# Moving one pair of token blocks of a two-layer GLU kernel into the joint seven-product stage

## The chip and the metric

One core of a Trainium2 chip. Times are microseconds of the device for one execution; runs of the same kernel are compared by their median.

## The reference

Channel attention on (6016, 256) tokens, then two gated layers with 1536 hidden units:

```python
def _attn_ref(q, k, v, tau):
    qn = q / (np.linalg.norm(q, axis=1, keepdims=True) + 1e-06)
    kn = k / (np.linalg.norm(k, axis=1, keepdims=True) + 1e-06)
    s = kn.transpose(0, 2, 1) @ qn / tau
    ...
    return (v @ a).astype(np.float32)

def _moe_ref(x, w_gate, w_val, w_out, rms_g):
    rms = np.sqrt(np.mean(x * x, axis=-1, keepdims=True) + 1e-06)
    xn = x / rms * rms_g
    g = xn @ w_gate
    silu = g * (1.0 / (1.0 + np.exp(-g)))
    val = xn @ w_val
    return (silu * val @ w_out).astype(np.float32)

def _moe2_ref(x, w_gate, w_val, w_out):
    gate = 1.0 / (1.0 + np.exp(-(x @ w_gate)))
    val = x @ w_val
    return (gate * val @ w_out).astype(np.float32)
```

## The kernel before, in words

The head computes the 256x256 attention matrix and multiplies the tokens by it. After that the program is two GLU layers on 12 blocks of 512 tokens (block 5 has 384), with hidden tiles f = 0 to 11 of 128 units. Every product is three fp32r matmuls of a high and a low half (`mm3`), so high and low halves of operands and weights are made on ScalarE ("hi": a copy) and VectorE ("lo": a difference).

Blocks go in pairs p = 0 to 5; the two halves of a pair are 512 tokens wide, those of pair 2 448. Three kinds of work stand in the program one after the other:

- **Plain**: 48 items (block, f) for blocks 0 to 3, the pairs 0 and 1 of layer one. An item has gate and value products in the banks `g` and `v` (12 matmuls, `plain_gv`), the output products of the item two before (6 matmuls, `out_mm`), and on the other engines gate, multiply, hi and lo (`plain_h`). The two layers' weights arrive as 64-bit floats and are converted here, 24 tiles (l, f), in the steps `units`, `shifted`, `whole`, `signed`, `size`, `rounded`, `guarded`, `high`, `low`, then `sums` of weight blocks on POOL with their own halves `s_high`, `s_low`, and stores to DRAM. `queue` lays the steps out after the table `ORDER` (a name with "-" is a step of the tile before), and `pump` puts a few behind each item's own work; `quota` says how many.
- **Alone** (`period`): pair 2 of layer one. A period is one f: the eight gate and value block products are made by seven, named 11, S1, P4, T2, 12, T3, S4, with copies of banks between them on ScalarE, and the output is made plainly by four products: 11 products, 33 matmuls. Weights stay in SBUF (`wh`, `wl`).
- **Joint** (`team_period`): pairs 3, 4, 5 of layer one, then pairs 0, 1, 3, 4, 5, 2 of layer two. The gate and value products are made as above. For the output, six hidden tiles make a team (half a pair); it takes 21 products (7 kinds x 3) for 24, made during the next half pair (`out_product`). So the first half pair, periods 0 to 5, has no output work (the step list `NONE`), and later ones have 10.5 products a period (`EVEN`, `ODD`). Weights are fetched from DRAM by `gw_load` (gate, value) and `ow_load` (output), operands by `pair_load`.

The program is in the order in which it is written (`manual_schedule`): each engine takes its instructions one after the other, DMAs are issued by SP, and accumulating DMAs by POOL. In the joint stage the step lists set the order: "cpA", "e5", "cpG", "cpD" are ScalarE's copies of banks, "sg" and "gate" its activations, "h1", "h0", "g1", "v1" VectorE's work. T3 writes to the bank that "cpG" reads, so T3 waits for "cpG".

Of the kernel before, what the change touches and what calls it, by code (L numbers as in the profile page):

```python
# [17 lines left out]
P = 128  # L18
SKEW = 2
# [6 lines left out]
def kernel(  # L26
# [35 lines left out]
    PLAIN = 2  # L62
    p0 = [starts[2 * p] * P for p in range(NP)]
# [37 lines left out]
    s3d = [dram.tile([P, 2, P], F32, name=f"s3d{f}") for f in range(NF)]  # L101
# [20 lines left out]
    def six(t):  # L122
        return t[:, A11:].rearrange("p (m c) n -> p m c n", c=KC)

    def conversion(l, f):
# [45 lines left out]
        def sums():  # L171
            t = w["t"]
            nc.sync.dma_start(out=rd[l][f // 2][:, f % 2 * 2 : f % 2 * 2 + 2], in_=t[:, OUT:])
            w["s3"] = cv2.tile([P, 1, P], F32, tag="s3", name="s3")
            nc.gpsimd.tensor_add(t[:, S1], t[:, A21], t[:, A22])
            nc.gpsimd.tensor_sub(w["s3"][:, 0], t[:, A11], t[:, A21])
# [3 lines left out]
        def high():  # L180
            if l:
                h = cv2.tile([P, NG, P], F32R, tag="w2h", name="w2h")
            else:
                h = wp.tile([P, NQ, P], F32R, tag=f"wh{f}", name="wh")
            own = slice(A11, NG if l else NQ)
            nc.scalar.copy(h[:, own], w["t"][:, own])
            w["h"] = wh[l, f] = h

        def low():
            if l:  # L190
                lo = cv2.tile([P, NG, P], F32R, tag="w2l", name="w2l")
            else:
                lo = wp.tile([P, NQ, P], F32R, tag=f"wl{f}", name="wl")
            own = slice(A11, NG if l else NQ)
            nc.vector.tensor_sub(lo[:, own], w["t"][:, own], f32(w["h"][:, own]))
            w["l"] = wl[l, f] = lo

        def sums_high():
            h = w["h"]
            nc.scalar.copy(h[:, :A11], w["t"][:, :A11])  # L200
            if l:
                w["3h"] = h[:, S3 : S3 + 1]
            else:
                w["3h"] = cv1.tile([P, 1, P], F32R, tag="s3h", name="s3h")
            nc.scalar.copy(w["3h"], w["s3"])

        def sums_low():
            h, lo = w["h"], w["l"]
            nc.gpsimd.tensor_sub(lo[:, :A11], w["t"][:, :A11], f32(h[:, :A11]))
            if l:  # L210
                w["3l"] = lo[:, S3 : S3 + 1]
            else:
                w["3l"] = cv1.tile([P, 1, P], F32R, tag="s3l", name="s3l")
            nc.gpsimd.tensor_sub(w["3l"], w["s3"], f32(w["3h"]))

        def stored():
            if l:
                nc.sync.dma_start(out=gd[l][f][:, 0], in_=f32(w["h"]))
                nc.sync.dma_start(out=gd[l][f][:, 1], in_=f32(w["l"]))
                del wh[l, f], wl[l, f]  # L220
            else:
                nc.sync.dma_start(out=s3d[f][:, 0], in_=f32(w["3h"])[:, 0])
                nc.sync.dma_start(out=s3d[f][:, 1], in_=f32(w["3l"])[:, 0])
# [6 lines left out]
        "-high units shifted", "-low", "whole signed", "size -s_high -s_low rounded", "guarded sums -stored"  # L230
# [3 lines left out]
    def queue(first, late):  # L234
# [7 lines left out]
        for i, tile_of in enumerate([*conversions, None]):  # L242
# [3 lines left out]
            for group in ORDER:  # L246
# [8 lines left out]
            if i + 2 < len(conversions):  # L255
                steps[-1].append(partial(load_w, *conversions[i + 2]))
# [135 lines left out]
    def pair_load(l, p, own):  # L392
# [8 lines left out]
        for i, (c, e) in ((B11, (0, 0)), (T3, (0, 1)), (B22, (1, 1)), (B21, (1, 0))):  # L401
# [39 lines left out]
    def plain_gv(it):  # L441
        b, f = it
        w = sizes[b] * P
        gv[it] = [gv_bank("g"), gv_bank("v")]
        for m, ps in enumerate(gv[it]):
# [878 lines left out]
```

## Time and profile before

| | |
|---|---|
| runs before | 1170.06 us median of 3 (1167.53 to 1170.07) |
| profiled execution | 1170.04 us, span 1168.3 us |
| TensorE | 1148.7 us busy (98%) |
| VectorE | 968.3 us (83%) |
| ScalarE | 890.2 us (76%) |
| POOL | 334.3 us (29%) |
| granted clock | 0.996 mean |

A timeline row gives start and duration in us, engine, source line, operation, out<-in by tile names, shapes, and in brackets the idle time before it and what ended it. The end of a matmul is modelled, so two starts tell more than one duration. A row by stage gives length, then busy time (and instructions) of TensorE, its weight loads, VectorE, ScalarE and POOL, then granted clock, DMA share and GB/s.

### The profile page before, as it was taken

How to read it: one execution, taken by the hardware profiler on the slowest of the kernel's cores; microseconds unless marked ns; L12 is line 12 of the kernel's file. 1: busy time of each engine (PE TensorE's matmuls, PEld its weight loads, DVE VectorE, ACT ScalarE, POOL GpSimd, SP SyncE). 2: the span in 40 equal slices, each digit the busy share in tenths (PEclk: the TensorE clock that was granted, in tenths of full speed). 3: DMA queues.
4: the chain of work that ended last, by engine and by line, in shares of the span. 5: the costliest groups of instructions: out<-in, count | busy, mean ns of one | idle time of the engine just before them, and what ended most of it. 6: DMA issues, size and time to landing. Idle time of an engine off the chain costs nothing.

```text
span 1168.3 us, 16678 instructions
## 1 busy us (share of the span) xinstructions
PE 1148.7 (98%) x5236; PEld 957.0 (82%) x5236; DVE 968.3 (83%) x1496; ACT 890.2 (76%) x1664; POOL 334.3 (29%) x398
## 2 busy tenths in 40 slices
PE   8899999999999999999999999999999999999998
PEld 7788788888898778888888788888888888888896
DVE  6798999886667688888888887888888888888877
ACT  6666788775577687887787887787787787787685
POOL 0043677454223322321321321311311321321121
PEclk9899999999999999999999999999999999999999
DMA  9663445867489989999999998998998998998995
GB/s 329 241 220 143 145 148 190 282 228 238 145 280 322 355 258 266 303 264 266 303 262 272 300 258 251 287 265 245 288 265 240 293 260 247 293 261 245 284 273 147
DMA packets 142856, 296.84 MB, mean 254 GB/s; under 512 B 13872, under 2 KB 53168, under 8 KB 142768
## 3 DMA queue, kind: packets, MB, share of 16 engines
q1 hardware_dynamic: 122032, 258.65, 65.6%
q0 software_dynamic: 20592, 37.00, 18.1%
q8 instruction: 41, 0.67, 0.2%
q14 instruction: 47, 0.39, 0.1%
q10 hardware_dynamic: 144, 0.13, 0.0%
HBM read 201.98 MB, written 56.75 MB: 221 GB/s over the span
## 4 chain that ended last, share of the span: by engine, by line
PE 84%; DVE 8%; DMA 4%; issue 2%; ACT 2%; POOL 1%; SPq 0%; DVEq 0%; POOLq 0%; ACTq 0%
PE g L107 12%; PE g L109 12%; PE g L108 12%; PE v L107 6%; PE v L108 6%; PE v L109 6%; PE y L108 5%; PE y L109 5%; PE y L107 5%; PE at L108 4%; PE at L107 4%; PE at L109 4%; DMA in<-in_q_dram 1%; PE y L973 1%; DVE xn L329 1%
## 5 line engine op out<-in xcount | busy, mean ns | idle before, releaser
L605 POOL DMA_DIRECT2D hs<-hs x143 | 124.7, 918 | 571.5 <-DVE hl L688 413.6
L688 DVE TENSOR_TENSOR hl<-hs,hh 128x512 fp32r<-128x512 f32 (+1 forms) x319 | 221.1, 704 | 25.1 <-ACT hh L657 24.2
L657 ACT CAST hh<-hs 128x512 fp32r<-128x512 f32 (+1 forms) x319 | 192.6, 615 | 25.7 <-PE at L109 6.5
L874 ACT COPY v<-g 128x512 f32<-128x512 f32 (+1 forms) x210 | 119.0, 567 | 63.1 <-PE g L109 59.8
L879 DVE TENSOR_TENSOR hs<-g,e 128x512 f32<-128x512 f32 (+1 forms) x105 | 71.5, 681 | 66.5 <-ACT v L874 65.6
L107 PE MATMUL g<-xh,gw 128*128 128x512 f32 x240 | 94.1, 392 | 0.7 <-DVE hs L879 0.6
L108 PE MATMUL g<-xl,gw 128*128 128x512 f32 x240 | 93.5, 389 | 0.0
L109 PE MATMUL g<-xh,gw 128*128 128x512 f32 x240 | 93.4, 389 | 0.0
L908 ACT ACTIVATE g<-g 128x512 f32<-128x512 f32 (+1 forms) x108 | 67.5, 625 | 30.4 <-DVE g L912 29.4
L107 PE MATMUL y<-hh,ow 128*128 128x512 f32 (+1 forms) x211 | 81.7, 387 | 0.2 <-issue 0.2
L108 PE MATMUL y<-hl,ow 128*128 128x512 f32 (+1 forms) x211 | 81.7, 387 | 0.0
L109 PE MATMUL y<-hh,ow 128*128 128x512 f32 (+1 forms) x211 | 81.6, 387 | 0.0
L874 ACT COPY g<-g 128x512 f32<-128x512 f32 (+1 forms) x105 | 61.3, 583 | 26.2 <-PE g L109 25.8
L912 DVE TENSOR_TENSOR g<-g,g 128x512 f32<-128x512 f32 (+1 forms) x105 | 70.3, 669 | 5.7 <-PE g L109 5.7
L883 ACT ACTIVATE sg<-v 128x512 f32<-128x512 f32 (+1 forms) x108 | 64.2, 594 | 7.5
L107 PE MATMUL g<-qh,gw 128*128 128x512 f32 (+1 forms) x171 | 66.5, 389 | 0.7 <-DVE hs L879 0.6
L109 PE MATMUL g<-qh,gw 128*128 128x512 f32 (+1 forms) x171 | 65.8, 385 | 0.0
L108 PE MATMUL g<-ql,gw 128*128 128x512 f32 (+1 forms) x171 | 65.8, 385 | 0.0
L108 PE MATMUL at<-hl,ow 128*128 128x512 f32 (+1 forms) x160 | 62.4, 390 | 0.6 <-DVE hl L688 0.6
L107 PE MATMUL at<-hh,ow 128*128 128x512 f32 (+1 forms) x160 | 62.2, 389 | 0.3 <-ACT hh L657 0.2
L109 PE MATMUL at<-hh,ow 128*128 128x512 f32 (+1 forms) x160 | 61.9, 387 | 0.0
L874 ACT COPY e<-g 128x512 f32<-128x512 f32 (+1 forms) x105 | 61.3, 584 | 0.4
(256 smaller groups left out, 3312.4 us busy)
## 6 DMA issues: line engine op xcount, KB each, us to landing
gw<-gd SPq DMA_DIRECT2D x216, 448.0 KB, 5.6
ow<-od SPq DMA_DIRECT2D x126, 384.0 KB, 5.4
hs<-hs POOLq DMA_DIRECT2D x128, 256.0 KB, 7.7
wraw<-in_w_dram SPq DMA_DIRECT2D x24, 768.0 KB, 5.3
od<-o SPq DMA_DIRECT2D x48, 256.0 KB, 4.6
vraw<-in_v_t_dram SPq DMA_DIRECT2D x11, 512.0 KB, 4.9
gd<-w2h SPq DMA_DIRECT2D x12, 448.0 KB, 2.6
gd<-w2l SPq DMA_DIRECT2D x12, 448.0 KB, 3.6
```

Source lines behind the costliest of these rows:

```text
L107: nc.tensor.matmul(ps, sh, mh, start=start, stop=False, skip_group_check=more)
L108: nc.tensor.matmul(ps, sh, ml, start=False, stop=False, skip_group_check=more)
L109: nc.tensor.matmul(ps, sl, mh, start=False, stop=stop, skip_group_check=more)
L329: nc.vector.tensor_scalar_mul(xn[b][:, i], ps[i // 2][:, i % 2], rs[:, i : i + 1])
L605: nc.gpsimd.dma_start(out=to, in_=t, accum_op=ALU.add)
L657: nc.scalar.copy(h, src)
L688: nc.vector.tensor_sub(lo, src, f32(h))
L874: nc.scalar.copy(new(name, make, *args), s[src])
L879: nc.vector.tensor_add(s["v1"], s["Z"], s["e5"])
L883: nc.scalar.activation(out=new("sg0", lambda: t), in_=s["A"], func=acts[l])
L908: "gate": lambda: nc.scalar.activation(out=pv["g1"], in_=pv["g1"], func=acts[pl]),
L912: "g1": lambda: nc.vector.tensor_add(s["g1"], s["g1"], s["B"]),
```

## The change

All pairs of layer one behind the plain stage become joint, in the order 3, 4, 5, 2; `period` goes. The plain stage therefore has to leave everything in DRAM that the joint stage fetches: gate and value weights (`store_plain`, `stored`), output weights (`store_out`) and the sums of output weights of layer one (`out_load`, `out_sums`, `out_high`, `out_low` behind items 22 to 41); those of layer two's first three pairs of tiles come behind periods 0, 2 and 4 (`soon_halves`). In the conversion the guard of a tile goes behind the next tile's sign step, raw weights have three buffers, and a load is asked for three tiles ahead (`FIRST` and `SECOND`, for the first four tiles that `queue` lays out, hold the old order). The last two plain items' output products run inside period 0 (`plain_out`), their banks are emptied there, and the two stores follow behind period 1. Of the first six periods the even ones use the `y` banks and the odd ones `g` (before: even `g`, odd `at`).

```diff
-    NQ = 9
-    S1, S2, S4, A11, A12, A21, A22, OUT = range(8)
-    S3 = A21
-    NG = OUT
+    NQ = 10
+    S3, S1, S2, S4, A12, A11, A22, A21, OUT = range(9)
+    NS = A12
+    NG = A21
+    NW = NQ - NS
...
-        t = cv2.tile([P, 3, KC, P, 2], U32, tag="wraw", name="wraw")
+        t = cv2.tile([P, 3, KC, P, 2], U32, tag="wraw", name="wraw", bufs=3)
...
     ORDER = (
-        "-high units shifted", "-low", "whole signed", "size -s_high -s_low rounded", "guarded sums -stored"
+        "units shifted",
+        "whole signed",
+        "size load -guarded -sums",
+        "-high rounded",
+        "-low -s_high -s_low -stored",
+    )
...
-            for group in ORDER:
+            if i + 3 < len(conversions):
+                now["load"] = partial(load_w, *conversions[i + 3])
+            for group in FIRST if i < first + 3 else SECOND if i == first + 3 else ORDER:
...
-    alone = [(0, PLAIN, f) for f in range(NF)]
-    joint = [(0, p, f) for p in range(PLAIN + 1, NP) for f in range(NF)]
+    joint = [(0, p, f) for p in (*range(PLAIN + 1, NP), PLAIN) for f in range(NF)]
     joint += [(1, p, f) for p in (0, 1, 3, 4, 5, 2) for f in range(NF)]
-    stream = alone + joint
...
     NONE = (
-        "11 S1 cpA gate h1 P4 third part1 T2 e5 12 flush h0 first"
-        " gw early part0 out out cpG ACT out sg T3 cpD out S4 end"
-        " DVE g1 v1"
+        "11 S1 cpA gate h1 P4 third T2 e5 12 flush h0 first gw early out out cpG ACT out sg T3 cpD out S4 DVE g1 v1 end"
     ).split()
...
         def bank(j):
-            return (at_bank, j) if n < HALF and n % 2 else (gv_bank, "g")
+            return (gv_bank, "g") if n >= HALF or n % 2 else (y_bank, j)
...
-            "S1": lambda: product(new("B", *bank(0)), it, T1, S1, True),
+            "S1": lambda: (product(new("B", *bank(0)), it, T1, S1, True), pv or out()),
...
-        end = len(items) - 5
+        now = len(items) - LATE
+        end = now - 6
+
+        def store_plain(f):
+            for e, t in enumerate((wh[0, f], wl[0, f])):
+                nc.sync.dma_start(out=gd[0][f][:, e, NS:], in_=f32(t[:, : NG - NS]))
+
+        def store_out(f):
+            g, j = divmod(f // 2, NJ)
+            for e, t in enumerate((wh[0, f], wl[0, f])):
+                nc.sync.dma_start(out=od[0][g][:, f % 2 * 2 : f % 2 * 2 + 2, e, j], in_=f32(t[:, 2 * KC :]))
...
+        for u, n in enumerate([22, 25, 28, 31, 34, 37]):
+            hook(n, out_load, 0, u)
+            hook(n + 2, out_sums, 0, u)
+            hook(n + 4, out_high, 0, u, 4)
+            hook(n + 4, out_low, 0, u, 4)
...
+        def plain_out(n):
+            b, f = items[n]
+            for c in range(KC):
+                out_mm(0, b // 2, b % 2, f, c)
+            if f == NF - 1:
+                for c in range(KC):
+                    evacuate(0, b // 2, b % 2, c, c, f32(hidden("hh")), True)
...
+            if n in SOON_AT:
+                slots[0].setdefault("end", []).append(partial(soon_halves, SOON_AT.index(n)))
...
-            if n < len(alone):
-                s = period(it, pv, outs)
-            elif it:
-                s = team_period(it, pv, n - len(alone), outs)
+            if it:
+                s = team_period(it, pv, n)
             else:
-                team_end(pv, n - len(alone))
+                team_end(pv, n)
+            if n == 1:
+                for fn in waiting:
+                    fn()
```

How the instructions stand now, at two places. First VectorE in the plain stage, one conversion and the plain items between (`v<-v,sg` and `hl<-v,hh` are a plain item's multiply and lo; `wbits<-wraw`, `wbits<-wraw,wbits`, `wbits<-wbits,wunits`, `wst<-wst,wbits`, `wl<-wst,wh` are shifted, signed, rounded, guarded, low). Before:

```order
L148 TENSOR_SCALAR wbits<-wraw 128x768
L195 TENSOR_TENSOR wl<-wst,wh 128x768
L478 TENSOR_TENSOR v<-v,sg 128x512
L158 SCALAR_TENSOR_TENSOR wbits<-wraw,wbits 128x768
L480 TENSOR_TENSOR hl<-v,hh 128x512
L163 ISA wbits<-wbits,wunits 128x1536
L166 SCALAR_TENSOR_TENSOR wst<-wst,wbits 128x768
L478 TENSOR_TENSOR v<-v,sg 128x512
```

and now:

```order
L149 TENSOR_SCALAR wbits<-wraw 128x768
L493 TENSOR_TENSOR hl<-v,hh 128x512
L159 SCALAR_TENSOR_TENSOR wbits<-wraw,wbits 128x768
L167 SCALAR_TENSOR_TENSOR wst<-wst,wbits 128x768
L491 TENSOR_TENSOR v<-v,sg 128x512
L164 ISA wbits<-wbits,wunits 128x1536
L493 TENSOR_TENSOR hl<-v,hh 128x512
L195 TENSOR_TENSOR wl<-wst,wh 128x768
```

The guard stood behind its own tile's rounding; now the guard of the tile before stands behind this tile's sign step, and the low half follows this tile's rounding.

Second ScalarE around the first joint period (`hh<-v` is the last plain item's hi, `v<-y`, `e<-y`, `g<-y` are cpA, e5 and cpG of period 0, `sg<-v` its sg, the second `v<-y` cpD). Only the new order has this seam:

```order
L492 CAST hh<-v 128x512
L387 CAST xh<-xl 128x512
L831 COPY v<-y 128x512
L831 COPY e_3353<-y 128x512
L522 COPY hh<-at 128x512
L831 COPY g_3368<-y 128x512
L840 ACTIVATE sg<-v 128x512
L831 COPY v<-y 128x512
L575 CAST o<-o 128x512 x2
L831 COPY v<-g 128x512
```

The emptying of a plain output bank (`hh<-at`) stands between e5 and cpG of period 0, and two splits of output weights (`o<-o`) stand behind its cpD, ahead of period 1's cpA.

## Rows read from the trace of the kernel before

**Rows 1.** First section of the page: busy time, share of the span, instructions.

```profile
PE 1148.7 (98%) x5236; PEld 957.0 (82%) x5236; DVE 968.3 (83%) x1496; ACT 890.2 (76%) x1664; POOL 334.3 (29%) x398
```

**Rows 2.** Busy time by stage, columns as told above.

```profile
387.18:421.81 34.63, 34.24 (x142) 25.84 (x141) 22.29 (x35) 23.47 (x44) 7.15 (x6) 1.00 1.00 341
...
465.19:551.86 86.67, 86.25 (x380) 70.76 (x379) 74.63 (x117) 69.70 (x128) 22.34 (x24) 1.00 0.96 279
1069.43:1109.46 40.03, 40.03 (x191) 35.50 (x190) 33.49 (x57) 29.98 (x58) 6.97 (x8) 1.00 0.95 273
119.00:200.00 81.00, 79.89 (x352) 65.99 (x352) 79.40 (x98) 64.70 (x111) 56.94 (x69) 1.00 0.51 166
200.00:280.00 80.00, 80.00 (x352) 65.72 (x351) 71.14 (x94) 58.74 (x103) 41.80 (x60) 1.00 0.72 246
```

**Rows 3.** Timeline of TensorE: plain matmuls nine apart, and the seventh joint period.

```profile
182.55 0.39 PE L107 MATMUL v<-qh,wh 128*128 128x512 f32 x1
...
184.59 0.39 PE L107 MATMUL at<-hh,wh 128*128 128x512 f32 x1
...
421.81 0.40 PE L107 MATMUL g<-qh,gw 128*128 128x512 f32 x1
```

**Rows 4.** Timeline of TensorE: first alone period's matmuls one and six, and a wait.

```profile
304.23 0.36 PE L107 MATMUL g<-xh,wh 128*128 128x448 f32 x1
...
305.24 0.36 PE L109 MATMUL g<-xh,wl 128*128 128x448 f32 x1
...
313.72 0.37 PE L109 MATMUL v<-xh,wl 128*128 128x448 f32 x1
314.68 0.44 PE L107 MATMUL at<-hh,wh 128*128 128x448 f32 x1 [0.60 <-DVE yo L509]
```

**Rows 5.** Timeline of TensorE and ScalarE in joint period 2: T2's end, cpG, T3.

```profile
402.95 0.39 PE L109 MATMUL g<-qh,gw 128*128 128x512 f32 x1
...
403.63 0.39 PE L109 MATMUL v<-qh,gw 128*128 128x512 f32 x1
404.02 0.50 PE L107 MATMUL g<-zh,gw 128*128 128x512 f32 x1
404.36 0.40 PE L108 MATMUL g<-zl,gw 128*128 128x512 f32 x1
...
403.38 0.59 ACT L874 COPY g<-g 128x512 f32<-128x512 f32 x1 [0.40 <-PE g L109]
```

**Rows 6.** Timeline of ScalarE in joint period 1: emptying of a bank, then cpG.

```profile
397.78 0.55 ACT L507 COPY yo<-y 128x448 f32<-128x448 f32 x1
398.29 0.59 ACT L874 COPY g<-at 128x512 f32<-128x512 f32 x1
```

**Rows 7.** Groups of VectorE from 119 to 200 us: signed, guarded, rounded.

```profile
L158 DVE SCALAR_TENSOR_TENSOR wbits<-wraw,wbits 128x768 uint32<-128x768 uint32 x12 | 12.6, 1047 | 0.0
L166 DVE SCALAR_TENSOR_TENSOR wst<-wst,wbits 128x768 f32<-128x768 f32 x11 | 12.2, 1112 | 0.3
...
L163 DVE CUSTOM_DVE_ANT_0 wbits<-wbits,wunits 128x1536 uint16<-128x1536 uint16 x11 | 10.6, 962 | 0.8
```

**Rows 8.** Timeline: lo of plain items 4, 16, 19; value product two items later.

```profile
130.01 0.68 DVE L480 TENSOR_TENSOR hl<-v,hh 128x512 fp32r<-128x512 f32 x1
...
133.59 0.39 PE L107 MATMUL v<-qh,wh 128*128 128x512 f32 x1
...
181.19 0.68 DVE L480 TENSOR_TENSOR hl<-v,hh 128x512 fp32r<-128x512 f32 x1
...
190.68 0.69 DVE L480 TENSOR_TENSOR hl<-v,hh 128x512 fp32r<-128x512 f32 x1
...
194.79 0.39 PE L107 MATMUL v<-qh,wh 128*128 128x512 f32 x1
```

**Rows 9.** Groups of POOL from 304 to 388 us: first sum of output weights.

```profile
L571 POOL TENSOR_TENSOR o<-o 128x128 f32<-128x128 f32 x9 | 6.4, 713 | 51.7 <-DVE o L563 31.4 <-PE g L109 20.3
```

**Rows 10.** Busy time by stage: the last pair.

```profile
1100.00:1140.00 40.00, 39.95 (x196) 36.27 (x195) 32.07 (x57) 32.41 (x66) 7.83 (x9) 1.00 0.99 281
```

More of the change, by code (lines that the diff above doesn't have):

```diff
@@ L181, in high @@
             if l:
-                h = cv2.tile([P, NG, P], F32R, tag="w2h", name="w2h")
-            else:
[L184 to L187, printed above, removed]
+                h = w["sh"] = cv2.tile([P, NG, P], F32R, tag="w2h", name="w2h")
+                nc.scalar.copy(h[:, NS:], w["t"][:, NS:NG])
+            else:
+                h = wh[l, f] = wp.tile([P, NW, P], F32R, tag=f"wh{f}", name="wh")
+                nc.scalar.copy(h, w["t"][:, NS:])
@@ L216, in stored @@
-        def stored():
[L217 to L223, printed above, removed]
+            if not l:
+                w["sh"] = cv2.tile([P, NG, P], F32R, tag="w2h", name="w2h")
+            h = w["sh"]
@@ new lines, in sums_high @@
+            nc.scalar.copy(h[:, :NS], w["t"][:, :NS])
+        def sums_low():
+            if not l:
+                w["sl"] = cv2.tile([P, NG, P], F32R, tag="w2l", name="w2l")
+            h, lo = w["sh"], w["sl"]
+            nc.gpsimd.tensor_sub(lo[:, :NS], w["t"][:, :NS], f32(h[:, :NS]))
+        def stored():
+            for e, t in enumerate((w["sh"], w["sl"])):
+                if l:
+                    nc.sync.dma_start(out=gd[l][f][:, e], in_=f32(t))
+                else:
+                    nc.sync.dma_start(out=gd[l][f][:, e, :NS], in_=f32(t[:, :NS]))
@@ L229 @@
     ORDER = (
-        "-high units shifted", "-low", "whole signed", "size -s_high -s_low rounded", "guarded sums -stored"
+        "units shifted",
[4 more added lines that the diff above has]
+    )
+    FIRST = (
+        "-high units shifted",
+        "-low",
+        "whole signed",
+        "size load -s_high -s_low rounded",
+        "guarded sums -stored",
+    )
+    SECOND = (
+        "-high units shifted",
+        "-low",
+        "whole signed",
+        "size load -s_high -s_low rounded",
+        "-stored",
     )
@@ L923, in team_period @@
         for step in (EVEN, ODD)[n % 2] if n >= HALF else NONE:
-            do.get(step, partial(at, step))()
+            if pv or step not in ("gate", "h1", "P4", "h0", "first"):
+                do.get(step, partial(at, step))()
         return s
@@ L1230 @@
                 slots.extend({} for _ in range(NF))
-                if n <= len(alone):
-                    done = outs[-1][:2]
-                    for e in range(2) if pv else (1,):
-                        point = slots[0].setdefault("ACT", []) if e and pv else slots[1].setdefault("early", [])
-                        point.extend(partial(evacuate, *done, e, c, c) for c in range(KC))
-                if n + NF < len(stream):
-                    nxt = stream[n + NF][:2]
+                if n + NF < len(joint):
+                    nxt = joint[n + NF][:2]
                     own = ((n // NF) % 2) == 1
@@ L1281 @@
             pv = s
-            outs = [(*it[:2], e, it[2]) for e in (1, 0)] if n < len(alone) else []
 def kernel(**inputs):
```

269 lines of the change are left out of this document (101 added, 168 removed), and 8 rows, old and new, of tables (EVEN, ODD).

## The prediction

> **What bounds the kernel now.** The first section of the page says it: TensorE is busy for nearly the whole span and VectorE is next [rows 1]. So I asked for busy time by stage, to see whether any stage is held by something else [rows 2]. In the plain stage (119 to 280 us) TensorE has no idle time to speak of, with VectorE right behind it, at 79.40 of 81 us in its first part. In a layer-one pair of the joint kind (465.19 to 551.86 us) 378 matmuls of 512 columns take 86.67 us. So the time is the number of matmuls times their spacing, plus the places where TensorE waits. The timeline of TensorE gives the spacing from start to start: 512 columns, 2.04 us over 9 matmuls, 0.2267 us [rows 3]; 448 columns, 1.01 us over 5, 0.202 us [rows 4]; I use 0.2025, since 126 x 0.2025 + 63 x 0.2267 = 39.8 us answers to the 40.03 us of the half pair at 1069.43 us [rows 2]. The granted clock is 1.00 in all these stretches, so no term of mine is one of the clock.
>
> The timeline then shows where layer one pays for more than its matmuls. The first matmul of the "alone" stage (pair 2) starts at 304.23 us [rows 4], the seventh joint period at 421.81 us [rows 3]: 117.58 us. Between them lie 396 matmuls of 448 columns (12 periods of 11 products, three matmuls each), 12 of 512 (output products of the last two plain tiles) and 126 of 512 (six joint periods of 7 products): 396 x 0.2025 + 138 x 0.2267 = 80.2 + 31.3 = 111.5 us. So 6.1 us here are waits, of a kind shown at 314.68 us, where the accumulation of a new output bank waits for the copy that empties it [rows 4].
>
> **The change, part by part.**
> *Products.* Pair 2 leaves the alone stage, is put behind pair 5 and gets its output product by seven for eight as well. Its output matmuls go from 12 x 4 x 3 = 144 to 42 x 3 = 126: 18 fewer, 18 x 0.2025 = 3.65 us. The rule in the Trainium skill, "TensorE: Matmul & The Clock Gate", section "Back-to-back issue gap", gives N/2.4 + 2.5 ns, 189 ns at 448 columns, and would make this 3.4 us; the trace's 202 ns decides.
>
> *The seam from plain to joint.* Now the first joint period follows the last plain tile. Its 138 matmuls of 512 columns cost 31.3 us as before. Of its waits two are readable. In each of the first joint periods T3 waits for the copy of T2's bank, with only "12" between: the last matmul of T2 starts at 402.95 us, the copy at 403.38, T3 at 404.02 in place of 403.86, and its next matmul 0.34 us later in place of 0.23: 0.27 us a period [rows 5]. Five periods keep that, 1.36 us; the bank swap alters which banks, not this chain. In period 0 output work lies between, but ScalarE's program now has the emptying of the last plain output bank ahead of that copy (the second piece of order above). So T3 waits for the last output matmul to drain (0.43 us from its start to the copy's, as at 402.95), for the emptying (0.51 us from its start to the next copy's [rows 6]) and for the copy (0.64 us to T3): 1.58 us instead of 0.23, a wait of 1.35 us. Bounds: nothing, if the copy gets through in time, and 1.9 us, if the emptying on VectorE is late as well by one operation; I take 1.35, since each piece has its row. The stores of these two banks wait for period 1; nobody reads that half of pair 1 until layer two.
>
> *Added to the first periods:* two splits each (1.1 us of ScalarE, 1.4 us of VectorE) behind periods 0, 2 and 4. ScalarE was busy 23.47 of 34.63 us there and VectorE 22.29 [rows 2]; ScalarE's idle 11.2 us over six periods take 3.3 us. I take nothing and keep 0 to 1.0 us.
>
> *Pair 2 as a joint pair:* 378 x 0.2025 = 76.5 us. The layer-one pair at 465.19 us took 86.67 for 378 x 0.2267 = 85.7: 1.0 us of waits [rows 2]. I charge pair 2 the same; bounds 0.2 (the half pair at 1069.43 us, 40.03 for 39.8) and 2.
>
> *The plain stage.* Removed there: the small conversions of S3. Added: splits of the layer-one output sums (6 on VectorE and ScalarE, 24 small POOL sums), stores of weights, DMAs on SP. Moved: the guard of a tile goes behind the next tile's sign step, and the third raw buffer lets a load go out three tiles ahead. VectorE's cover is the thing to check. I counted its operations up to each plain tile's "hl" in both orders, with the means of this stage. They agree up to tile 3; at tile 4 the new order is one guard later, 1.11 us [rows 7], where the old one has a lead of 2.90 us (hl done at 130.69, the bank's next matmul at 133.59) [rows 8]. From 6 to 16 it is equal or earlier by up to 0.26 us; tile 16 has the thinnest lead, 0.68 us (181.87 against 182.55) [rows 3, 8]. At 19 it is 1.83 us late (one more sign step and rounding, 1.05 + 0.96, less 0.18 for a smaller split) against a lead of 3.42 us (191.37, 194.79) [rows 7, 8]. No lead is used up. After 200 us VectorE has 8.9 us of 80 idle [rows 2], and the six splits take 4.1 (0.68 each, as an hl). POOL and SP have no work that TensorE waits for here except through those leads. I take zero, 0 to 2 us.
>
> *The sum.* Old stretch 117.58. New: 31.3 + 1.36 + 1.35 + 0.2 (spacing a little wide in these periods) = 34.2, and 76.5 + 1.0 = 77.5: 111.7. The gain is 5.9 us, 3.65 of it matmuls and the rest waits of the alone stage that go with it. The profiled execution took 1170.04 us (span 1168.3), the median is 1170.06, so both give 1164.1 us. All other pairs, the last one among them, have the same matmuls.
>
> **The rivals.**
> *A seam without the new wait* (the emptying hidden): 1.35 us less and perhaps half of pair 2's waits, 1162.3 us. For it: VectorE has the other bank and ScalarE is idle right before. Against it: the order on ScalarE. Chance 0.12.
>
> *The plain stage loses its lead.* POOL gets 24 sums there, at most 0.71 us each [rows 9], 17 us. If they held VectorE for as long as they run, it would have 17 + 4.1 us more work between 200 and 280 us against 8.9 idle, and end 12 us late against a lead like that of tile 19, 3.42 us: at worst 8.8 us of waits, 1173 us, and at half of that 1168.5, which I take for its time. Against it: between 119 and 200 us POOL was busy 56.94 us and VectorE 79.40 of the same 81 [rows 2], so they ran side by side. The Trainium skill, "SBUF — State Buffer", section "SBUF: two separate sides", says that GpSimd and a VectorE operation with two SBUF inputs lock one another out for a whole instruction; by that this rival would be the likely one, and those two busy times do not bear it out for the mix as a whole. Chance 0.13.
>
> *The seam or the splits cost double:* waits of the first periods as large as those of the alone stage, 6 us instead of 2.9, 1167 us. Chance 0.09.
>
> *The transfers fall behind in pair 2, and it gets slower.* At 448 columns a period is shorter, but its gate and value weights are as many bytes. The last pair moved 281 GB/s [rows 10]; pair 2 has in addition the next pair's operands, four loads of 256 KB in 77 us, 14 GB/s: 295. If the queues hold only R, pair 2 stretches by 77 x (295/R - 1): at 263 GB/s 9.4 us, which is 1173.5. It decides from about there down. Against it: 341 GB/s between 387.18 and 421.81 us, 279 in an ordinary pair, and no wait of TensorE for a weight load in either [rows 2]. Chance 0.05.
>
> *It does not do what it says:* no gain from the moved pair because its waits are as large as the alone stage's; that is inside the third rival.
>
> **How the numbers follow.** Forecast 1164.1 us, chance 0.61, its own range 1162.8 to 1166.2 (the bounds above, not all at their worst). With the first rival below and the second and third above, 1161.8 to 1168.5 holds eight in ten. 0.3% is 3.5 us, about what a measurement can tell: faster means under 1166.6. That takes the forecast nearly whole (0.59), the first rival (0.12) and a little of the others (0.06): 0.77. Slower, over 1173.6: 0.05. The rest, 0.18, is within.
>
> **What would show it.** Right: the stretch from the last plain tile to the seventh joint period is about 34 us; one wait of some 1.3 us before T3 of period 0, put down to a ScalarE copy; pair 2 takes 77 to 78 us; no new TensorE wait between 120 and 300 us. Wrong: TensorE waits for VectorE or a weight in the plain stage; joint periods of pair 2 longer than 6.5 us with waits for "gw" or "ow"; or a matmul spacing that differs from 0.2267 and 0.2025 us for whole stretches.

## The result and the profile after

The changed kernel takes 1177.63 us (median of 4, 1175.63 to 1180.3); the kernel before, run beside it, 1168.8. The ratio is 1.0076, 95% interval 1.0055 to 1.0096: slower by some 9 us, where 1164.1 was forecast, 1166.2 was the top of the forecast's own range and 1168.5 that of the wider one. The profiled execution took 1180.3 us, its span is 1178.5 us, 10.2 more than before. One execution among all the kernels below, one of the seven of the changed kernel without the splits, took 1911 us, and the ratio given there leaves it out.

The first section of its page shows no engine that became the bound: TensorE is at 98% again, with 18 matmuls fewer [rows 1].

```profile
PE 1150.0 (98%) x5218; PEld 955.3 (81%) x5218; DVE 985.2 (84%) x1524; ACT 892.1 (76%) x1654; POOL 339.3 (29%) x390
```

Busy time by stage tells where the 10.2 us are. The columns are those of [rows 2]. Before, the plain stage (first plain product to the first alone one) and the first half of layer two's first pair were:

```profile
104.81:304.23 199.42, 197.43 (x869) 161.49 (x869) 175.48 (x230) 144.46 (x255) 110.50 (x142) 1.00 0.56 185
...
638.64:682.72 44.08, 43.83 (x190) 35.16 (x189) 37.99 (x60) 35.30 (x63) 12.52 (x12) 1.00 0.98 286
```

After: the plain stage (to the first joint product), pair 3's first half, the two halves of pair 2, and layer two's first half pair.

```profile
103.68:316.73 213.05, 203.78 (x868) 162.77 (x869) 180.72 (x234) 142.77 (x237) 120.03 (x150) 0.98 0.78 262
316.73:353.83 37.10, 34.08 (x139) 25.12 (x138) 26.13 (x40) 26.40 (x49) 10.57 (x10) 1.00 0.77 242
570.36:612.08 41.72, 40.31 (x190) 35.41 (x189) 37.22 (x60) 32.09 (x62) 12.93 (x12) 1.00 1.00 298
612.08:650.75 38.67, 38.67 (x191) 35.41 (x190) 31.98 (x58) 32.01 (x65) 7.00 (x8) 1.00 0.97 276
650.75:693.43 42.68, 42.55 (x190) 35.17 (x189) 35.74 (x59) 33.45 (x61) 12.53 (x12) 1.00 0.97 279
```

The plain stage, which I had priced at zero, takes 213.05 us for 199.42: 13.6 us more for the same products. Counted from start to start, 5.1 us of that are waits before value products between 187 and 284 us, 2.9 a single wait at 307.6 us, and 3.0 two stretches at half the clock, shown at the end. The part on which my gain rested, pair 3's first half and pair 2, takes 37.10 + 41.72 + 38.67 = 117.5 us where the old stretch took 117.58 and 111.7 was forecast. The head is 1.1 us shorter, and the rest, layer two's first half pair above all, 2.2 us. 13.6 - 1.1 - 0.1 - 2.2 = 10.2.

**How a wait in the plain stage comes about.** Between 240 and 290 us TensorE stands before the value product of a tile at 242.9, 255.7, 260.9, 270.5 and 283.5 us; its timeline shows two of them:

```profile
255.66 0.39 PE L110 MATMUL g<-qh,wl 128*128 128x512 f32 x1
256.85 0.50 PE L108 MATMUL v<-qh,wh 128*128 128x512 f32 x1 [0.80 <-DVE hl L493]
...
260.87 0.39 PE L110 MATMUL g<-qh,wl 128*128 128x512 f32 x1
262.44 0.50 PE L108 MATMUL v<-qh,wh 128*128 128x512 f32 x1 [1.19 <-DVE hl L493]
```

The value bank is free when hl of the tile ahead is done. So read backwards from hl at 256.11, on VectorE, ScalarE and POOL, in the same microseconds:

```profile
248.86 0.95 DVE L159 SCALAR_TENSOR_TENSOR wbits<-wraw,wbits 128x768 uint32<-128x768 uint32 x1
...
250.32 1.87 DVE L167 SCALAR_TENSOR_TENSOR wst<-wst,wbits 128x768 f32<-128x768 f32 x1
252.92 0.78 DVE L579 TENSOR_TENSOR ol<-o,oh 128x512 fp32r<-128x512 f32 x1 [0.73 <-POOL wst L175]
253.63 1.21 DVE L164 CUSTOM_DVE_ANT_0 wbits<-wbits,wunits 128x1536 uint16<-128x1536 uint16 x1
254.77 0.69 DVE L491 TENSOR_TENSOR v<-v,sg 128x512 f32<-128x512 f32 x1
255.37 0.54 DVE L192 TENSOR_TENSOR w2l<-wst,w2h 128x384 fp32r<-128x384 f32 x1
256.11 0.69 DVE L493 TENSOR_TENSOR hl<-v,hh 128x512 fp32r<-128x512 f32 x1 [0.20 <-ACT hh L492]
257.14 2.24 DVE L390 TENSOR_TENSOR ql<-ql,qh 128x512 fp32r<-128x512 f32 x2 [0.34 <-ACT qh L387]
```

```profile
251.42 0.91 ACT L137 ACTIVATE wst<-wraw 128x768 f32<-128x768 f32 x1 [1.10 <-POOL w2l L207]
252.23 0.61 ACT L575 CAST oh<-o 128x512 fp32r<-128x512 f32 x1
```

```profile
248.96 1.17 POOL L595 TENSOR_TENSOR o<-o 128x128 f32<-128x128 f32 x1
250.09 1.30 POOL L207 TENSOR_TENSOR w2l<-wst,w2h 128x512 fp32r<-128x512 f32 x1
```

POOL makes the low part of a tile's sums until 251.39. ScalarE's size step (L137) of the tile two further needs the buffer that this reads (there are two), so it stands 1.10 us. Behind it in ScalarE's line is `oh`, the rounding of a split output sum; VectorE's guard ends at 252.19, but `ol`, next in its line, needs `oh`, which ends at 252.84: VectorE is idle for 0.73 us. (The row names POOL L175 as the releaser; that started at 252.28 and ended no earlier than 252.7, so what `ol` waited for is `oh`.) Rounding, product, hh and hl follow in line, and TensorE waits 0.80 us by its row, 0.96 by its starts. One tile on, two subtractions of the next block (2.24 us) meet the lateness that is left, 1.19 us. At 283.5 us the same three instructions stand in the same order; at 270.5 us ScalarE waits for POOL at another place, the rounding of the sums (L201, 0.82 us), again with `oh` next in line. The small wait at 242.9 us, 0.21 us, has the same pattern: 0.82 us at L201 (238.23 us), `oh` behind it, and VectorE idle for 1.33 us before `ol`.

### The profile page after: what moved, and what is told of

Same layout as the page of the kernel before. It is cut to its first block, busy times and chain, and to the rows that moved or that the text cites. A ratio compares the mean times of both kernels' runs of the same rounds, so it can differ in the third digit from the quotient of the medians.

```text
span 1178.5 us, 16723 instructions
## 1 busy us (share of the span) xinstructions
PE 1150.0 (98%) x5218; PEld 955.3 (81%) x5218; DVE 985.2 (84%) x1524; ACT 892.1 (76%) x1654; POOL 339.3 (29%) x390
## 4 chain that ended last, share of the span: by engine, by line
PE 75%; DVE 9%; DMA 7%; issue 4%; POOL 3%; ACT 2%; SPq 0%; DVEq 0%; POOLq 0%; ACTq 0%
PE g L108 11%; PE g L110 11%; PE g L109 11%; PE v L108 5%; PE v L109 5%; PE v L110 5%; PE y L108 5%; PE y L109 5%; PE y L110 5%; PE at L109 4%; PE at L108 3%; PE at L110 3%; DMA in<-in_q_dram 2%; DMA gw<-gd 1%; DVE xn L338 1%
## 5 line engine op out<-in xcount | busy, mean ns | idle before, releaser
L626 POOL DMA_DIRECT2D hs<-hs x159 | 138.8, 922 | 625.2 <-DVE hl L709 458.8
L709 DVE TENSOR_TENSOR hl<-hs,hh 128x512 fp32r<-128x512 f32 (+1 forms) x355 | 242.9, 695 | 27.7 <-ACT hh L678 25.8
L678 ACT CAST hh<-hs 128x512 fp32r<-128x512 f32 (+1 forms) x355 | 212.7, 610 | 27.7 <-PE at L110 7.1
L831 ACT COPY v<-g 128x512 f32<-128x512 f32 (+1 forms) x234 | 131.5, 562 | 67.4 <-PE g L110 63.9
L836 DVE TENSOR_TENSOR hs<-g,e 128x512 f32<-128x512 f32 (+1 forms) x117 | 79.0, 675 | 74.0 <-ACT v L831 73.4
L108 PE MATMUL g<-xh,gw 128*128 128x512 f32 x285 | 112.3, 394 | 1.0 <-DVE g L869 0.8
L110 PE MATMUL g<-xh,gw 128*128 128x512 f32 x285 | 111.3, 391 | 0.7 <-DMA gw<-gd 0.7
L109 PE MATMUL g<-xl,gw 128*128 128x512 f32 x285 | 111.2, 390 | 0.0
L108 PE MATMUL y<-hh,ow 128*128 128x512 f32 (+1 forms) x235 | 90.5, 385 | 0.2 <-issue 0.2
L109 PE MATMUL y<-hl,ow 128*128 128x512 f32 (+1 forms) x235 | 90.5, 385 | 0.0
L110 PE MATMUL y<-hh,ow 128*128 128x512 f32 (+1 forms) x235 | 90.5, 385 | 0.0
L108 PE MATMUL at<-hh,ow 128*128 128x512 f32 (+1 forms) x178 | 68.7, 386 | 0.2 <-ACT hh L678 0.2
L110 PE MATMUL at<-hh,ow 128*128 128x512 f32 (+1 forms) x178 | 68.5, 385 | 0.0
```

The costliest lines, as they stand in the source:

```text
L108: nc.tensor.matmul(ps, sh, mh, start=start, stop=False, skip_group_check=more)
L109: nc.tensor.matmul(ps, sh, ml, start=False, stop=False, skip_group_check=more)
L110: nc.tensor.matmul(ps, sl, mh, start=False, stop=stop, skip_group_check=more)
L626: nc.gpsimd.dma_start(out=to, in_=t, accum_op=ALU.add)
L678: nc.scalar.copy(h, src)
L709: nc.vector.tensor_sub(lo, src, f32(h))
```

## The experiments

I held two theories after this. A: the new order of a weight's conversion leaves hl late, because what POOL makes is needed sooner after it is asked for. D: transfers that the change put ahead of the first joint pair's operands make these late. Times below are medians; the kernel before stood at 1167.7 to 1169 us beside them. They moved by over 1 us between sets of runs on different chips, so I give the ratio to them with each time. The first plain product starts anywhere from 101.0 to 105.6 us in fourteen profiles, so I compare stages from their own start.

### The old order alone

```diff
-            for group in FIRST if i < first + 3 else SECOND if i == first + 3 else ORDER:
+            for group in FIRST:
```

> Undoes one part: every tile is converted in the order that the first three tiles have, so the guard follows its own tile's rounding and the split of the sums comes four steps behind the sums in place of two. Theory A (in the changed kernel ScalarE waits for POOL's sums before it can split them, 13.2 us in 12 waits between 120 and 320 us, the plain item's hi behind it is late, and TensorE waits for hl): those 12 waits all but go, the waits of TensorE for hl (6.2 us in the gaps between 183 and 285 us) fall below 2 us, and the time falls by 4 to 6 us, to about 1172. Rival B (hl is late because of the splits of output weights that were put behind items 22 to 41, not because of the order): the gaps before 205 us go (1.3 us), those from 240 us on stay, and the time falls by less than 2 us.

1168.91 us, ratio 1.0015 [1.0001, 1.0028]: 8.7 us come back with one line (7.1 by the ratios), more than either expectation had. ScalarE no longer waits for POOL's sums, and TensorE's rows of waits for hl from 120 to 300 us shrink. Of the changed kernel these waits, and VectorE's group `ol` from 119 to 290 us with its idle time ahead:

```profile
ACT w2h L201 <- POOL wst L178: 13.2, 12, 1.5
PE v L108 <- DVE hl L493: 3.7, 6, 1.2
...
L579 DVE TENSOR_TENSOR ol<-o,oh 128x512 fp32r<-128x512 f32 x5 | 5.0, 994 | 4.8 <-POOL wst L175 2.2 <-DMA rd<-wst 1.3 <-DMA o<-rd 1.3
```

Of this one, with its plain stage:

```profile
PE v L108 <- DVE hl L493: 0.8, 3, 0.4
...
L579 DVE TENSOR_TENSOR ol<-o,oh 128x512 fp32r<-128x512 f32 x6 | 5.1, 857 | 0.0
```

```profile
100.98:305.05 204.07, 199.28 (x868) 161.01 (x869) 182.87 (x233) 140.42 (x235) 117.21 (x150) 1.00 0.81 272
```

The stage row says more: VectorE is busy for 182.87 of 204.07 us here and for 180.72 of 213.05 in the changed kernel. It was not overloaded by the change; it stood, 4.8 us of it before `ol`, where it does not stand at all here. Not all of the 9.0 us between the two plain stages are waits for hl, though: the single wait at 307.6 us shrinks from 2.93 us to 0.88, with 0.69 in a second place, and this trace has no stretch at half the clock.

### The plain output weights stored early

```diff
-            hook(at[2 * PLAIN - 1, f], store_out, f)
+            hook(at[1, f] + 2, store_out, f)
```

> Moves one part: the 24 stores of layer one's output weights are issued as soon as a tile is converted and not behind items 36 to 47. Theory C (pair 3's operands land late, 12.8 us of waiting on POOL, because these stores and the first three weight fetches fill the queue just ahead of them: DMA share 1.0 at 280 to 310 us; ScalarE then stands at the split of the operands and the gate behind it is late): the operands land at least 4 us earlier, the gap of 2.9 us at 307.6 us goes, and with it the stretch at half clock behind it; 3 to 5 us faster, about 1173. Rival D (the three weight fetches alone fill the queue): POOL's wait shrinks by less than 2 us and the gap stays over 2 us.

1177.87 us, ratio 1.0081 [1.0064, 1.0099]: nothing. POOL's wait for the operands falls from 12.8 to 10.3 us and TensorE's stand of 2.93 us at 307.6 us to 0.52 and 0.70, but other places take it up (1.79 us at 186 us, and 1.37 us in place of 0.44 before T2 of the first joint period). This is neither expectation: the stores have a part in the delay, 2.5 us of POOL's wait, but taking it away earns no time.

### The first gate and value weights fetched later

```diff
-            hook(at[2 * PLAIN - 1, n] + 4, gw_load, n)
+            hook(at[2 * PLAIN - 1, n] + 8, gw_load, n)
```

> Moves one part: the fetches of the first three periods' weights are issued behind items 44, 45, 46 in place of 40, 41, 42, so behind pair 3's operands on SP. Theory C, with the stores as the larger part (3.1 MB of stores against 2.7 MB of fetches between items 36 and 47): the operands land 1 to 3 us earlier, the gap at 307.6 us shrinks but stays, 1 to 2 us faster. Rival D (the fetches alone): the gap goes, 3 to 5 us faster, as much as the early stores bring or more. If the fetches are then late themselves, TensorE waits for gw at the start of period 0.

1173.4 us, ratio 1.0049 [1.0029, 1.0068]: 4.2 us less than the changed kernel (3.2 by the ratios), as rival D had it. The waits from 295 to 320 us, first before (285 to 306 us there), then after, then here:

```profile
POOL xs L410 <- DMA xl<-xd: 5.4, 1, 5.4
```

```profile
POOL xs L419 <- DMA xl<-xd: 12.8, 1, 12.8
ACT xh L387 <- POOL xs L419: 9.1, 2, 6.7
...
PE g L108 <- ACT sg L490: 2.8, 1, 2.8
```

```profile
POOL xs L419 <- DMA xl<-xd: 8.8, 1, 8.8
ACT xh L387 <- POOL xs L419: 5.1, 2, 2.7
```

The chain is: operands late, POOL's first sum late, ScalarE's rounding of it late, and in ScalarE's line behind that the gate of the plain tile. In the changed kernel's timeline of ScalarE:

```profile
306.56 0.62 ACT L387 CAST xh<-xs 128x512 fp32r<-128x512 f32 x1 [6.66 <-POOL xs L419]
309.60 0.62 ACT L387 CAST xh<-xs 128x512 fp32r<-128x512 f32 x1 [2.42 <-POOL xs L419]
310.12 0.59 ACT L490 ACTIVATE sg<-g 128x512 f32<-128x512 f32 x1
```

TensorE's stand at 307.6 us is gone here. So D is a second cause, of its own place. That POOL's wait is still longer than before (8.8 against 5.4 us) no longer shows at TensorE.

### The last plain bank emptied behind the copy for T3

```diff
+        emptied = deque()
+
+        def empty():
+            while emptied:
+                emptied.popleft()()
...
-                for c in range(KC):
-                    evacuate(0, b // 2, b % 2, c, c, f32(hidden("hh")), True)
+                emptied.extend(
+                    partial(evacuate, 0, b // 2, b % 2, c, c, f32(hidden("hh")), True) for c in range(KC)
+                )
...
+            if n == 0:
+                slots[0].setdefault("ACT", []).append(empty)
```

> Moves one part: the two last plain output banks are emptied behind cpG of period 0 and not ahead of it. Theory (the wait of 1.49 us before T3 of period 0 is ScalarE's emptying ahead of cpG, as forecast): the wait goes, the rest stays, 1.2 to 1.5 us faster, 1176.2. Rival (T3 waits as long for the cpG copy because ScalarE is late for another reason): less than 0.4 us faster.

1177.06 us, ratio 1.008 [1.0065, 1.0095]. The time moves by less than can be told, which is neither expectation; the wait goes. TensorE at T3, in the changed kernel and here:

```profile
322.53 0.39 PE L110 MATMUL at<-hh,wl 128*128 128x512 f32 x1
324.13 0.50 PE L108 MATMUL y<-xh,gw 128*128 128x512 f32 x1 [1.22 <-ACT g L831]
```

```profile
321.49 0.39 PE L110 MATMUL at<-hh,wl 128*128 128x512 f32 x1
321.72 0.39 PE L108 MATMUL y<-xh,gw 128*128 128x512 f32 x1
```

1.60 us from start to start, and 0.23 here: 1.37 us, for which the forecast had 1.35. Pair 3's first half falls from 37.1 to 35.3 us.

### The three together, and with the new order

Old order, late fetch, late emptying, all three edits as above:

> The changed kernel with three of its parts undone or moved at once: the old order of a weight's conversion, the gate and value weights of the first joint periods asked for four tiles later, and the emptying of the last plain output bank placed behind the copy that T3 of the first joint period waits for. If the three costs stand side by side, what is left of the first experiment's small waits goes: the two of 0.98 and 0.81 us ahead of the seam (operands of the first joint pair late) and the 1.49 us at T3, so about 1165.5 us against 1168.9 with the old order alone, and a little under the kernel before. If the costs overlap (the same matmuls would have waited for the next thing anyway), it stays at 1168 to 1169, the same as with the old order alone.

1165.35 us, ratio 0.9976 [0.9963, 0.9989]: faster than the kernel before by 3.2 us, the best of this study. Its plain stage still takes 2.9 us more than before, about half of it a stretch at half the clock at 121 us:

```profile
104.81:307.15 202.34, 199.56 (x869) 162.50 (x869) 185.16 (x236) 142.68 (x238) 117.60 (x150) 0.99 0.80 272
```

The same with the new order:

> The changed kernel, new conversion order kept, with the fetch of the first gate and value weights four tiles later and the emptying of the last plain bank behind the copy that T3 waits for: what the combination of three edits has, less the old order. If costs add, it takes 1177.6 - 4.2 - 0.6 = 1172.8 us, or with the T3 wait whole 1171.9, and the order is worth 6.5 to 7.5 us beside them. If the late fetch was only making up for the order (fewer loads while conversions run late), it takes 1169 us or less.

1172.9 us, ratio 1.0034 [1.0019, 1.0049]. The costs add: the order is worth 7.5 us with the other two out of the way, and the late fetch does not make up for it. The ratios make the order 6.8 us. The profiled executions place only a part of it: the plain stage takes 206.03 us here and 202.34 in the combination, 3.7 us more, and the four waits before value products that stand here (at 255, 260, 270 and 283 us) come to 3.7 us from start to start. The spans lie 6.2 us apart; 0.9 us of the rest is in pair 3's first half, and the remainder in small differences of the head and of later stages, which one profile of each can't tell from chance.

### Why the order costs: the rounding moved to POOL

```diff
-            nc.scalar.copy(h[:, :NS], w["t"][:, :NS])
+            nc.gpsimd.tensor_copy(h[:, :NS], w["t"][:, :NS])
```

> The changed kernel, with its new conversion order whole, but the rounding copy of the four sums (s_high) runs on POOL, behind POOL's own sums, and no more on ScalarE. The theory says that the loss is ScalarE standing in line at this copy for POOL: then the waits of ScalarE for POOL's sums leave the trace, hl comes in time, and the kernel takes 1168 to 1171 us, near the 1168.9 of the old order. The rival says that the loss is the later guard on VectorE itself, whoever rounds the sums: then the waits before the hl products stay and it takes 1175 to 1178 us. A third way: POOL, with 18 more copies, becomes late itself for the stores and for the operands of the first joint pair, and it takes more than 1178 us.

1176.62 us, ratio 1.0078 [1.0059, 1.0098]: a miss for my theory as I had put it, and inside the range of the rival, the later guard itself. The wait of ScalarE for the sums is gone and nothing came back. Its waits show why, and sent me to the buffer that stands at the head of the chain told above:

```profile
ACT wst L137 <- POOL w2l L207: 7.8, 4, 2.5
ACT wst L137 <- DMA rd<-wst: 6.7, 4, 2.6
```

In the changed kernel the first is 2.9 us in three waits. ScalarE still stands for POOL, now at the next buffer, and POOL has more to do ahead of releasing it. So the particular wait was not the cause; that ScalarE waits for POOL at all, with something urgent behind, may be. This run leaves the rival standing; the two runs without the splits below speak against it, since they keep the later guard and have no wait for hl.

### The new order on the kernel before

```diff
-            for group in ORDER:
+            for group in FIRST if i < first + 3 else SECOND if i == first + 3 else ORDER:
```

(with ORDER, FIRST and SECOND as in the change, less "load")

> The kernel before with one part of the change alone: the guard of a tile behind the next tile's sign step, and with it POOL's sums and the copy of the sums at the places that the change gives them. Alone stage, loads, splits and stores are as before. If this order is the loss and needs nothing else of the change, it takes 1173 to 1177 us, 5 to 9 more than the kernel before, with ScalarE waiting 10 us or more for POOL's sums between 120 and 300 us. If the order costs only together with what else the change put into this stage (six splits of output sums and 24 POOL sums), it takes 1167 to 1170 us.

1170.48 us against 1168.5, ratio 1.0017 [1.0004, 1.003]: 2 us, just above the second expectation and far from the first. ScalarE waits for POOL's sums even longer than in the changed kernel (18.9 us against 13.2), and TensorE hardly feels it:

```profile
ACT w2h L200 <- POOL wst L178: 9.7, 10, 1.2
ACT wh L200 <- POOL wst L178: 9.2, 7, 1.5
```

So the order costs mainly together with something else that the change put into this stage.

### Without the splits of output sums

```diff
-            odd[l, i] += [cv2.tile([P, 512], F32, tag=t, name=t) for t in ("oh", "ol")]
+            odd[l, i] += [odd[l, i][0]] * 2
+            return
...
+        if l:
+            nc.vector.tensor_sub(lo.bitcast(F32R), odd[l, i][0], h)
```

> The changed kernel without the six splits of layer one's output sums in the plain stage: ScalarE's copies and VectorE's subtractions are left out, and the sums are stored as they are; POOL still makes them. The order alone cost the kernel before 2 us and costs the changed kernel 8.7, so something else of the change must work with it. Theory: it is these splits, which stand on VectorE in front of the product whose result the value bank waits for; then TensorE's waits between 240 and 290 us (4.5 us in the changed kernel) go and the time falls to 1172 to 1174 us, and to 1169 if the late operands of the first joint pair follow from them too. Rival: it is POOL, whose sums are needed two steps after they are asked for; then the waits stay and it takes 1176 to 1178 us.

1173.57 us, ratio 1.004 [1.0021, 1.0058]: 4.1 us less. No row of TensorE waiting for hl is left from 120 to 300 us. ScalarE still waits 13.2 us for POOL's sums; only the split, ScalarE's copy and VectorE's subtraction, does not stand behind that wait any more. Which of the two matters was not tried apart. The wait for the operands at 302.4 us stays (2.13 us and matmuls at half clock behind it).

### Without POOL's sums

```diff
-            nc.gpsimd.tensor_add(t[:, S1], t[:, A21], t[:, A22])
-            nc.gpsimd.tensor_sub(t[:, S3], t[:, A11], t[:, A21])
-            nc.gpsimd.tensor_sub(t[:, S2], t[:, S1], t[:, A11])
-            nc.gpsimd.tensor_sub(t[:, S4], t[:, A12], t[:, S2])
...
-            nc.scalar.copy(h[:, :NS], w["t"][:, :NS])
+            nc.scalar.copy(h[:, :NS], w["t"][:, NS : 2 * NS])
```

(and the same columns in the subtraction of L207)

> The changed kernel without POOL's four sums of every weight tile: the four TensorTensor operations are left out, and the rounding and the low part read four of the weight's own parts in their place, so the same copies, subtractions and stores remain. If POOL's sums between the guard and their rounding are the loss (on ScalarE's line, and through the buffer that is freed when POOL is done), the waits for POOL go and the time falls to 1168 to 1171 us. If the six splits on VectorE and ScalarE are the loss, it stays at 1175 to 1178 us. POOL also makes the operands of the first joint pair, but these wait for a transfer, so nothing is expected there.

1173.17 us, ratio 1.0038 [1.0025, 1.0052]: 4.5 us less, between the two expectations. With POOL's sums gone and the splits in place, most of the waits go too; the row is of the changed kernel less its sums, from 120 to 300 us, and the changed kernel's stands under the old order above.

```profile
PE v L108 <- DVE hl L489: 1.2, 3, 0.7
```

The two runs say the same from both ends: it takes both, POOL's work late in ScalarE's line and a split behind it.

### Without the splits, late fetch, late emptying

The edits of the runs above, new order kept.

> New conversion order kept, the six splits of layer one's output sums left out (the sums are stored as they are), the fetch of the first gate and value weights four tiles later and the emptying of the last plain bank behind the copy that T3 waits for. With the old order and the splits in place this combination took 1165.4 us, with the new order and the splits 1172.9. If the order costs through the splits alone, the waits between 240 and 290 us are gone and it takes 1166 to 1167.5 us, that is the 1165.4 and up to 2 us that the order cost the kernel before. If the order has a cost of its own beside the splits, as the run without POOL's sums suggests, it takes 1169 to 1171 us, with waits of TensorE for hl left before 240 us.

1166.13 us, ratio 0.9983 [0.9971, 0.9995]: 6.8 us under the same kernel with the splits, and 0.8 over the one with the old order and the splits: the first expectation. Without the splits the new order is nearly free, with ScalarE's wait for POOL's sums at 12.2 us:

```profile
ACT w2h L201 <- POOL wst L178: 12.2, 13, 1.5
```

### The stores of split sums behind the fetch of weights

On top of the combination of three edits:

```diff
+    after_gw = []
...
-            nc.sync.dma_start(out=dst, in_=t.rearrange("p (u n) -> p u n", u=4))
+            put = partial(nc.sync.dma_start, out=dst, in_=t.rearrange("p (u n) -> p u n", u=4))
+            if l and i < NJ:
+                after_gw.append(put)
+            else:
+                put()
...
+            if n in (1, 3, 5):
+                while after_gw:
+                    after_gw.pop(0)()
```

> As the combination of the three edits, and in addition the stores of the split output sums in the first joint periods are issued one period later, behind the fetch of the gate and value weights, so that SP does not stand at a store that waits for ScalarE while the weights of the period after next are due. The trace of the changed kernel has a wait of 0.95 us of TensorE for such weights at 336 us; if SP's place in line is its cause, it goes and the time falls by 0.9 us against the combination, to about 1164.6 us. If the weights wait for their buffer (freed by the period before) and not for SP, the wait stays and the time with it.

1168.39 us, ratio 0.9993 [0.9981, 1.0004]: 3 us worse than the combination, where 0.9 better was expected. The wait for "gw" that was meant is gone, and another, longer one has come near it; the combination's, then this kernel's:

```profile
325.65 0.50 PE L110 MATMUL g<-xh,gw 128*128 128x512 f32 x1 [0.79 <-DMA gw<-gd]
```

```profile
326.51 0.50 PE L108 MATMUL g<-xh,gw 128*128 128x512 f32 x1 [1.44 <-ACT v L836]
```

The profiled executions differ by only 0.6 us, with a head 1.4 us shorter here and pair 3's first half 1.9 us longer (37.1 against 35.2), so the seam is where this kernel loses. Why the copy of v is late there was not followed further.

## Why the prediction was wrong

- **The step that failed** is "The plain stage", and in it the words "No lead is used up" and "I take zero, 0 to 2 us"; the stage took 13.6 us more. I counted VectorE's operations up to each tile's hl and compared their sum with the lead, and set the six splits (4.1 us) against 8.9 us of VectorE's idle time after 200 us. Both are sums of work. The waits came from the order of the lines: an operation on VectorE that needs ScalarE, behind an operation on ScalarE that needs POOL. None of these engines was full; VectorE was busier with the old order, and the waits for hl fell to 0.8 us. The order of the program would have told it: on ScalarE `oh` of a split follows the size step, and the new order frees that step's buffer later.
- **"POOL and SP have no work that TensorE waits for here except through those leads"** was false in its second half as well. SP issues the gate and value weights of two joint periods ahead of the first joint pair's operands, and behind these operands, through POOL and ScalarE, stands the gate of a plain tile. The late fetch alone gave 4.2 us.
- **The rival that named the plain stage** had the place and not the mechanism. It let POOL hold VectorE, ended at 1173 us at worst and got 0.13. Its "at most 0.71 us each" was a mean [rows 9]; in the changed kernel such a sum took from 0.46 to 1.17 us. I spoke against it with two busy times, 56.94 and 79.40 of the same 81 us [rows 2], "so they ran side by side". That does not follow, since a row's duration can hold a wait inside: the guard took 0.94 us alone (at 262.31 us) and 1.87 at 250.32, beside the POOL operation that ended at 251.39, and 251.39 + 0.94 = 252.33 is near its end, 252.19. The rule that I set aside, from the Trainium skill, "SBUF — State Buffer", section "SBUF: two separate sides" (one of the two gets the shared port for a whole instruction), agrees with this row.
- **Which stretching counted.** That of the guard cost nothing: at 0.94 us the guard would have ended at 251.26, and `ol` had to wait for `oh` until 252.84 all the same. By the rows it was the other direction that counted, VectorE holding POOL. The sum L595 at 248.96 us took 1.17 us (0.46 at 260.51); it began 0.10 us after VectorE's sign step and ended 0.41 us after the next VectorE operation started at 249.72. Ahead of the wait at 283.5 us POOL's low part took 2.02 us for 1.30, begun 0.30 us after a sign step; ahead of those at 242.9 and 270.5 the first sum took 1.11 us for 0.46, begun about 0.15 us after a rounding. By these rows 0.65 to 0.72 us of each of ScalarE's four waits (1.10, 0.89, 0.82 and 0.82 us) is stretching, an estimate that no run tests alone: the one without POOL's sums took the stretching and the line of waits away together. With the old order POOL's operations are stretched as much (its low part takes 1.51 us in the mean for 1.45), and ScalarE does not wait for them.
- **The seam** was right in mechanism: T3 waited 1.37 us for 1.35, put down to ScalarE's copy, and five periods kept their 0.27. It was under-sized by what I had not listed: 0.44 us before T2 of period 0 and two waits of about a microsecond, one at 336 us for weights that SP had issued late (it stood at the stores of a split), one at 352 us for VectorE's work on a bank. 37.1 us for 34.2.
- **Pair 2 as a joint pair** came to 80.4 for 77.5 us. 1.5 us of that is a slip in the term's place and not in the sum: a team's output product runs in the half pair that follows, so 63 matmuls of pair 2's first half are pair 5's, 512 wide, and 63 x (0.2267 - 0.2025) = 1.5 us. Pair 2's own run in layer two's first half pair, 42.68 us for 44.08. Most of the rest is one wait, 1.57 us over the spacing where I had charged 1.0 for the whole pair:

```profile
596.24 0.39 PE L110 MATMUL at<-hh,ow 128*128 128x512 f32 x1
598.04 0.47 PE L108 MATMUL g<-qh,gw 128*128 128x448 f32 x1 [1.41 <-DVE hs L836]
```

- **The products** were right: 18 fewer, at the spacings used. With the order, the fetch and the emptying out of the way, the combination shows a part of the gain: 3.2 us, against the kernel before beside it at 1168.5, of the 5.9 forecast, and its plain stage loses 2.9 us all the same. That its 1165.35 us lies 1.2 us over the forecast is partly luck, since the forecast counted from 1170.06.

What adds up: the order with the splits 7.5 us, the late operands 4.2, the emptying 0.6, together the 12.3 us between the changed kernel and the combination (each of the three good to one or two us). By the ratios it is 6.8 for the order and 4.9 for the other two together. Of the order's share 3.7 us are shown as waits in the plain stage; where the rest is lost stays open.

## What to carry to other kernels

An idle share doesn't say that an operation is free: write down for each added operation what it waits for, what stands ahead of that on the other engine's line, and what stands behind it on its own. A chain that crosses three engines in program order can hold the last one even where each has time to spare: 1.10 us on ScalarE became 0.73 on VectorE and 0.96 on TensorE here. When a change makes something due sooner after it is asked for, look for the buffers that are then freed later, and for the first queue in which a fetch for later stands ahead of an operand for now.

## What the runs showed of the hardware

A short wait of TensorE can be followed by microseconds at half the clock. After the wait of 1.8 us in a stream of matmuls at 118 us the spacing is 0.427 us for seven matmuls in place of 0.2267 (1.2 GHz for 2.4), 1.4 us lost; after the wait at 307.6 us again, and the granted clock from 300 to 316 us is 0.89.

```profile
118.06 0.40 PE L109 MATMUL g<-ql,wh 128*128 128x512 f32 x1
119.90 0.50 PE L110 MATMUL g<-qh,wl 128*128 128x512 f32 x1 [1.44 <-DVE wl L195]
...
120.48 0.63 PE L109 MATMUL g<-ql,wh 128*128 128x512 f32 x1
120.91 0.63 PE L110 MATMUL g<-qh,wl 128*128 128x512 f32 x1
```

```profile
300.00:316.00 16.00, 13.23 (x51) 10.11 (x50) 6.30 (x9) 4.75 (x9) 10.26 (x12) 0.89 0.96 314
```

The length of the wait does not decide alone. A wait of 1.83 or 1.84 us from start to start stands at this place in ten of the kernels. Half the clock follows it in five (the changed kernel, the combination, the same with the stores behind the fetch, the same with the new order, and the changed kernel without the splits) and in none of the other five. One of these, with the last bank emptied late, has the same program up to there as the changed kernel. What decides was not tried.

The scatter between executions goes with the clock. The changed kernel took 1180.3 and 1179.02 us at a mean granted clock of 0.993, and 1176.24 and 1175.63 at 0.997 and 0.998. In the fourteen profiles the first plain product starts at 101.0 and 101.4 us where the granted clock of the first 101 us is 1.00, at 102.8 to 103.7 where it is 0.98, and at 103.7 to 105.6 where it is 0.97.
